# A delta-rule attention and two expert layers in one kernel: key blocks of the first eight items transposed by TensorE instead of by DMA

## The chip, the cores and the metric

One core of one Trainium2 chip runs the whole program. The metric is the device time of one execution in microseconds (us); lower is better. The kernel runs five engines side by side: TensorE (PE in the rows), VectorE (DVE), ScalarE (ACT), GpSimd (POOL), and SyncE (SP), which here only issues DMAs.

## The reference, cut to what matters

```python
def _attn_ref(q, k, v, beta):                # 4 x 8 heads, 768 steps, head size 48
    k_n = k / (norm(k) + 1e-06)
    for t in range(S):
        y[t] = q[t] @ state
        v_old = state applied to k_n[t]
        state = state + beta[t] * outer(k_n[t], v[t] - v_old)

x = y as [3072, 384]
h = x @ w_in;  g = h * clip(h + 3, 0, 6) / 6;  x = g @ w_out      # 384 -> 2048 -> 384
logits = x @ w_gate                          # 8 experts, the best one for each token
out[mask] = gate_w * (relu(x[mask] @ w1[e]) @ w2[e])              # 384 -> 1024 -> 384
```

## The kernel before, in words

The recurrence is computed in chunks of 64 steps. There are 12 chunks (`NS`), and the 32 pairs of batch and head lie in two halves of 16, so there are 24 items (`NI`), item `it` being chunk `it // 2` and half `it % 2`. A half holds eight head numbers `u` of two batches `bb`; `bb` 0 lies on rows 0 to 63 and `bb` 1 on rows 64 to 127. All values go as pairs of a high and a low part (fp16 or fp32r), and each product is made of three matmuls.

For each item, the keys are normalised (`n_stream`, `k_stream`, lines 396 to 435) and written as two 64-column blocks on the diagonal of a tile `Kbd` (128 x 2 x 8 x 128, eight such tiles, `bd_rows` line 373). From `Kbd` come two transposed copies, both by DMA transposes on SP's queue:

- `KTb` (`kt_stream`, line 558), for the products with the queries (`pP`) and with the state (`pR`).
- `KG` (`kg_stream`, line 441), for the product of the keys with themselves. `keysT` (line 437) says where it lies: items 0 and 1 use `KTb`, items 2 and 3 the tiles `QTb`, which no query needs yet, and from item 4 on there is one tile `KG`, so that the transpose of an item waits until the product of the item before has read it.

`g_stream` (line 453) makes the product `pG` of an item with 48 matmuls of 64x64 on two quarters of the array, and ScalarE copies it to `Dt` (four copies) and `MC`. For each group of four items, `t_stream` (line 484) transposes `Dt` on VectorE into `Bt`, scales it, and clears `Xp` in PSUM. `s_stream` (line 501) solves the triangular system of the group on VectorE: 31 steps of two instructions each (`sub`, `Xp`). `z_stream` (line 518) turns the solution into `TT`, and with the products `pZ` into `W2`; `wc_stream` makes `W1`. `chain` (line 677) then carries the state from chunk to chunk (`pR`, `pW`, `pS`), `o_stream` makes the attention output (`pO`), `x_stream` transposes it to `xT`, and `m_stream` (line 877) runs seven of the sixteen slices of the first expert layer on it (`ph`, `py`), while the weights of these slices are converted from 64-bit words by `wi_stream` and `wo_stream` (`nws`; for each piece four operations on VectorE, two on ScalarE and one on GpSimd). The other nine slices, the routing and the second expert layer come after the attention, from about 480 us on (lines 1121 to 1436); the change doesn't touch them.

The order of the work up to there is written out by hand. Each of 31 streams is a generator that yields its instructions in turn; a string `ORDER` (line 959) of 2,998 letters names, letter by letter, the stream whose next entry is emitted, and `drive` (line 926) emits them. A letter stands for one instruction, or for a list of matmuls that belong together. `need` only says which entries must have been emitted earlier; it makes no wait on the chip. Each engine works through its own instructions in this order, and waits where the data need it. `take` hands out one of three PSUM banks. In the string `m` is `g_stream`, `n` is `k_stream`, `c` is `kg_stream`, `d` is `kt_stream`, `l` is `s_stream`, `t` is `m_stream`.

In the trace nearly all of this has the line 36, that of the helper which records each operation, so that the tiles' names tell the instructions apart.

Of the kernel before, what the change touches and what calls it, by code (L numbers as in the profile page):

```python
# [9 lines left out]
FP16 = mybir.dt.float16  # L10
# [61 lines left out]
def kernel(ctx: ExitStack, tc: tile.TileContext, q, k, v, beta, w_in, w_out, w_gate, w1, w2, out):  # L72
# [50 lines left out]
    idq = const.tile([128, 32], FP32, name="idq")  # L123
    onef = const.tile([128, 128], FP32, name="onef")
# [85 lines left out]
    with ExitStack() as ax:  # L210
# [46 lines left out]
        NKG = 1  # L257
        NTT = 1
# [21 lines left out]
        def zero_stream(eng):  # L280
# [7 lines left out]
            yield from need(("K", 3))  # L288
# [99 lines left out]
        def kl_stream():  # L388
            for s in range(NS):
                yield "next"  # L390
                if s > 1:
                    yield from need(("K", 3), ("kn", 2 * s - 4), ("kn", 2 * s - 3))
                ks[s] = yield from load_step(k, s, "kr", 2)
                done.add(("kl", s))
# [42 lines left out]
        def keysT(it):  # L437

            return KTb[it] if it < 2 else QTb[it - 2] if it < 4 else KG[it % NKG]

        def kg_stream():

            for it in range(2, NI):
                yield "next"
                yield from need(("KB", it))
                if it >= NKG + 4:
                    yield from need(("G", it - NKG))
                kb, ktb = Kbd[it % NRK], keysT(it)
                kb.read(it), ktb.write(it)
                yield transposed(ktb, kb)  # L450
                done.add(("K", it))

        def g_stream():

            for it in range(NI):
                g, j = divmod(it, 4)
                yield "next"
                yield from need(("K", it) if it > 1 else ("KT", it))
# [5 lines left out]
                kg = keysT(it)  # L464
                kt = kg.t
                kg.read(it)
                if it >= NMG:
                    yield from need(("Z", it - NMG))
                p = yield from take("pG", kt)
                p_ = p.rearrange("p (u t) -> p u t", t=64)  # L470
                yield [o for u in range(H) for o in halves(lambda r: (p_[r, u], [kt[r, x, u, r] for x in range(2)], [kt[r, x, u, r] for x in range(2)]), True, True)]
                kg.read(it)
# [100 lines left out]
        def ql_stream():  # L573
            for n in range(NS // 2):
                yield "next"
                yield from need(("qf", n - 1) if n else ("K", 3))
# [349 lines left out]
        def drive(streams):  # L926
# [33 lines left out]
            "jjaaaajkjkkkpbrbbbbbbkpbbrqqsrpobsrbrbrbqsbsbqsqrjsqbqqqqnsqrqsosposqr1n1n0nr0onsnosrrnnrsnqrsnnqqso",  # L960
            "osrnqnssnqnsqpdssnrrmssmsnrmsqqnnrdrncmskqmmmmmmjorsqmmsmmrscjqmmkmmskksaomkrmmmrmskmsmmkmksksmassbs",
            "rsrhbrhhbrabarblrbllqrlsbbrlqbspsssrlbbqqlbsbbblb6nnslqlsrsllrlrnnnnllllslnlslsllqslerclnnsmrlsnsnlr",
            "nnsnesrlemllarksllellelllelallslslrbelslbcnnlmmbrlslrmsmlqlaamllresmelrsmlbsmllqlbrebbrlnmlllnllmnlb",
            "crblmisknbrimrmbsmkbbk7fsmmiesibrmemmsqfiscfmq2sbsibimfimsridimmiis3m7i322mhr331h1hf1f1eels20s10qfe1",
            "llsfr031lsl100l60qflf0enr1li2eqninsn10idqelseleliii2in0l1i1ls0i2l41li30l1l40lfe3sngfngql5efgl005l3f1",
            "gs2sc1ls0gnfl1egaa0dl0e1tltnt0s8tnn8lsltl01m0lltetmmpt1lsct0ltntmnmtnmtelpttbttt0sltl1smltl14mfnltlb",
            "ld7s1mtlllc104ltttbtmtlttqtstmqttt1l0ttll1ttmltsm1nntltentststtllmlltt0llqlfaa0nltl0ntfllmbmfqtmmttl",
            "ttqtli10bqtitecstfqtgmg5tpt5tbgmbqmgmitgpqbgtqbmmb7qib2b222bietbmq3biib6tetiq3mt0t0tmt0ttmftt3th02ti",
            "0hqqi0ehttqetttftidl0qt2f3iql0qlqtlllltlin1n1tfeqlnntttttt1tll0elnnll2i4etlelet1l01td1l3tttitl98t24i",
            "1iq31t1tel10nnct3ttntttt0ifllif0i0tfm1ltmt3mnftmn1laa8liilttttimt0tltqd0m0ttlttgmfl0tg1e0gteclfel500",  # L970
            "llq5l1l0efggmltfqg1ltmntdtt1tlpnllltlq08t80lmtnptt4tnllnt4lt1lttltltltttmm1t07tqtqaall1tl0tbl1llltct",
            "0tt1tntl1tll1qlbenttltetttt1nmblntitbiftbtttttmf1ti9mm60ebctqmmmmbtttqt1qq2tttq31bmf2t1t2bttg5itbtgi",
            "ebqq3q52gigg3igtitq030itbmbptbbitmb0imit0mt0i0qp71mnet211eqqt0e0n2qfmteeeenetmt440tt1hh1tef0hd9tqtnt",
            "tqt81fntn08ttqflq0llllfeqllqllltid1tfl21tlqlii0tlt1tit3tt0tltnt1tflttttct2i0300tlit1li3t0ett0tnt1lfi",
            "fllitt0mlillft0tm3lt1qltfl0ntttmnltttldmmtltt1glql5gm5gttgllq4aenablg0fg1tlln0lll1nftm8ttl1tttntltnd",
            "4ttc7tltt11lllmtm1mlmtm0tn1tetlleppblmatlllllcttnttltlt1ltl0qlbttmtt8tlftqtn0ttn1ttlftlqtnitqtft1ttm",
            "t0tttatibqbfqmtmiqbtqbq8ctmmmt1tt1bbttttimiq21t3qitbt69g57igib3i2532egbegitbttgi2qg1pq3emimbi1bmm0b1",
            "e1n0t10mpmtm3t10h02tttheft101hftf1tqqtl3ifllel0tt0telltql0tln4dd10el8qt4eqliqnn2nttte2le1qltfqfel0tt",
            "icltnf1if20l1l0tltitln3tint10ltqtf0l8t0dqntlnfl0llettltttt10mtt0nml0limltmtlmttqitltt0ttn0lll3ttmilt",
            "inetctnttttnnt8llmltllqlttglql5mg5glltt0m9mm10g1l1ttgfmlg1tm1ttllt1t1plplml4qtnlllqttnnttctfn4ltllld",  # L980
# [486 lines left out]
```

## Time and profile before

| | us |
|---|---|
| median of 3 runs | 992.2 |
| lowest, highest run | 988.83, 997.2 |
| the profiled execution, its own time | 993.86 |
| its span in the trace | 992.1 |
| busy: PE, DVE, ACT, POOL | 884.6, 594.8, 568.6, 430.7 |
| PE busy in 0 to 105 us, 105 to 390, 390 to 992 | 34.63, 262.69, 587.27 |
| DVE busy in the same stretches | 94.64, 252.70, 247.47 |

Times in the rows are microseconds from the start of the span unless marked ns. A row of the timeline gives the start, the time to the end of the last of its instructions, the engine, what is written from what, and in brackets how long the engine had sat idle and who released it. `xN` is a count. Rows of matmuls that run one behind the other are merged, so that 48 of them in 1.49 us follow each other every 31 ns, though each one alone is longer. PEclk is the clock granted to TensorE as a share of the full one.

### The profile page before, as it was taken

Reading aid. Unit: us, or ns where it says so; the run is one execution under the profiler, and the core shown is the slowest. Engines: PE = TensorE matmul, PEld = TensorE weight load, DVE = VectorE, ACT = ScalarE, POOL = GpSimd, SP = SyncE. Lnnn points to the kernel's source line nnn. Section 1 sums busy time; section 2 is a strip of 40 time slices with the busy share of each in tenths; the row PEclk is TensorE's granted clock in tenths of the full one; section 3 lists DMA queues with packets and bytes.
Section 4 is the critical chain, followed back from the end, with each engine's and each line's share of the span. In section 5 each row is a group of like instructions: output and inputs, shape, how many; then the busy total and the mean of one; then the engine's idle time right before and its main releaser. Section 6 shows DMA issues by size and latency. Waiting matters only on the chain.

```text
span 992.1 us, 27636 instructions
## 1 busy us (share of the span) xinstructions
PE 884.6 (89%) x11454; PEld 817.0 (82%) x11454; DVE 594.8 (60%) x1612; ACT 568.6 (57%) x1195; POOL 430.7 (43%) x445
## 2 busy tenths in 40 slices
PE   1423898999999999999999999999999999999997
PEld 1323897888888988999778899899899999999996
DVE  7999998988989898564575545554543221222221
ACT  4648888888798877666557333333324452455521
POOL 5354465544646434334343104303105935755751
PEclk9999799999999999999989999999999999999999
DMA  8998888899988875574465323422117634534500
GB/s 144 183 156 162 136 143 146 167 151 181 155 147 175 161 149 150 135 221 157 127 194 180 125 64 100 147 78 98 65 50 269 217 101 147 153 121 131 175 21 21
DMA packets 255080, 138.89 MB, mean 140 GB/s; under 512 B 199587, under 2 KB 239845, under 8 KB 254944
## 3 DMA queue, kind: packets, MB, share of 16 engines
q1 hardware_dynamic: 247120, 118.82, 53.0%
q0 software_dynamic: 7280, 17.41, 5.3%
q8 instruction: 91, 1.49, 0.6%
q10 hardware_dynamic: 544, 0.80, 0.2%
q14 instruction: 45, 0.37, 0.1%
HBM read 71.56 MB, written 35.50 MB: 108 GB/s over the span
## 4 chain that ended last, share of the span: by engine, by line
PE 64%; DVE 18%; issue 6%; ACT 6%; POOL 3%; DMA 1%; SPq 1%; POOLq 0%; ACTq 0%; DVEq 0%
PE ph L1296 11%; PE ph L1087 9%; PE ph L36 7%; PE py L36 6%; PE py L1312 4%; PE py L1311 4%; PE py L1310 4%; PE pz L1075 3%; PE pz L1077 3%; PE pz L1076 3%; PE pO L36 3%; DVE Xp L36 2%; DVE sub L36 2%; PE pW L36 2%; DVE nws L36 1%
## 5 line engine op out<-in xcount | busy, mean ns | idle before, releaser
L1091 DVE SCALAR_TENSOR_TENSOR hL<-ph,hH 128x384 fp32r<-128x384 f32 (+6 forms) x64 | 36.1, 564 | 163.5 <-ACT hH L1090 163.5
L36 POOL TENSOR_TENSOR gL<-t,gH 128x256 fp32r<-128x256 f32 x84 | 64.9, 772 | 129.7 <-ACT gH L36 117.4
L1090 ACT ACTIVATE hH<-ph 128x384 fp32r<-128x384 f32 (+6 forms) x64 | 31.7, 495 | 105.2 <-PE ph L1087 105.2
L36 PE MATMUL ph<-xTH,wiH 128*128 128x256 f32 x252 | 76.9, 305 | 14.4 <-DVE t L36 13.7
L1299 ACT ACTIVATE t<-ph,half 128x512 f32<-128x512 f32 x54 | 37.2, 689 | 78.0 <-PE ph L1296 77.8
L1256 POOL DMA_INDIRECT slots<-row,di x24 | 23.9, 997 | 125.1 <-DVE di L1248 119.6
L1300 DVE SCALAR_TENSOR_TENSOR t<-t,ph 128x512 f32<-128x512 f32 x54 | 37.1, 687 | 66.7 <-ACT t L1299 66.4
L1075 PE MATMUL pz<-a2H,hH 128*128 128x384 f32 (+1 forms) x216 | 73.2, 339 | 0.4 <-ACT hH L1090 0.4
L1076 PE MATMUL pz<-a2L,hH 128*128 128x384 f32 (+1 forms) x216 | 72.4, 335 | 0.0
L1077 PE MATMUL pz<-a2H,hL 128*128 128x384 f32 (+1 forms) x216 | 72.4, 335 | 0.0
L1108 POOL DMA_INDIRECT out_dram<-yo,rw x29 | 28.0, 966 | 100.6 <-ACT yo L1107 96.4
L36 PE MATMUL ph<-xTL,wiH 128*128 128x256 f32 x252 | 70.6, 280 | 0.0
L36 PE MATMUL ph<-xTH,wiL 128*128 128x256 f32 x252 | 70.6, 280 | 0.0
L36 PEld LDWEIGHTS ph<-xTH,wiH 128*128 128x128 f32 x252 | 47.5, 189 | 24.4 <-DVE t L36 24.1
L1304 DVE TENSOR_TENSOR gL<-t,gH 128x512 fp32r<-128x512 f32 x54 | 46.6, 863 | 32.7 <-ACT gH L1303 32.5
L36 DVE TENSOR_TENSOR Xp<-Xp,sub 128x31 f32<-128x31 f32 (+15 forms) x186 | 63.7, 342 | 2.4
L36 PE MATMUL py<-woH,gH 128*128 128x392 f32 x168 | 63.5, 378 | 1.1 <-ACT gH L36 1.1
L36 DVE TENSOR_TENSOR sub<-Bt,Xp 128x31 f32<-128x31 f32 (+15 forms) x186 | 61.7, 332 | 2.8 <-POOL Bt L36 0.5
L148 POOL TENSOR_TENSOR a2L<-r,a2H 128x384 fp32r<-128x384 f32 x64 | 62.5, 1007 | 0.0
L148 POOL TENSOR_TENSOR a1L<-r,a1H 128x512 fp32r<-128x512 f32 x48 | 60.4, 1300 | 0.1
L36 PE MATMUL py<-woH,gL 128*128 128x392 f32 x168 | 58.2, 346 | 0.5 <-POOL gL L36 0.5
L1087 PE MATMUL ph<-yTL,a1H 128*128 128x384 f32 (+5 forms) x168 | 58.3, 347 | 0.0
(321 smaller groups left out, 3122.4 us busy)
## 6 DMA issues: line engine op xcount, KB each, us to landing
r<-in_moe_w_dram SPq DMA_DIRECT2D x32, 768.0 KB, 4.5
slots<-zrow SPq DMA_DIRECT2D x8, 784.0 KB, 6.4
stage<-in_moe_w_in_dram SPq DMA_DIRECT2D x16, 384.0 KB, 3.9
stage<-in_moe_w_out_dram SPq DMA_DIRECT2D x16, 384.0 KB, 3.4
row<-ypart SPq DMA_DIRECT2D x6, 784.0 KB, 4.3
ysave<-row SPq DMA_DIRECT2D x6, 784.0 KB, 3.6
rw<-slots SPq DMA_DIRECT2D x24, 196.0 KB, 3.1
kr<-in_k_dram SPq DMA_DIRECT2D x24, 192.0 KB, 4.2
```

Of the source, the lines that this page charges most:

```text
L36: return self.fn(*self.a, **self.k)
L148: in_order(pool.tensor_tensor(dst[1], src_ap, dst[0].bitcast(FP32), ALU.subtract))
L1075: pe.matmul(o, hh[:, ts_], a2[0][:, fp], start=fp == 0, stop=False)
L1076: pe.matmul(o, hh[:, ts_], a2[1][:, fp], start=False, stop=False)
L1077: pe.matmul(o, hl[:, ts_], a2[0][:, fp], start=False, stop=fp == KF2 - 1)
L1087: pe.matmul(ph, a1[a][:, c, fs], xt[x][:, c, 0:n], start=k == 0, stop=k == 3 * KD - 1)
L1296: pe.matmul(ph, wi(a, f)[:, c], xt[x][:, c], start=n == 0, stop=n == 3 * KD - 1)
L1299: act.activation(t_, ph, ACTF.Relu, bias=half, scale=1.0 / 6.0)
L1304: dve.tensor_tensor(gL, t_, gH.bitcast(FP32), ALU.subtract)
L1310: pe.matmul(o, gh[:, ts_], wo(0, fp), start=fp == 0, stop=False)
L1311: pe.matmul(o, gh[:, ts_], wo(1, fp), start=False, stop=False)
L1312: pe.matmul(o, gl[:, ts_], wo(0, fp), start=False, stop=fp == NF2 - 1)
```

## The change

Items 0 to 7 no longer get a DMA-transposed copy for `pG`. Instead, `pt_keys` transposes the 32 blocks of 64x64 of an item's `Kbd` on TensorE (fp16, against a 64x64 identity `id16` that ScalarE copies out of `ident` at the start) into one PSUM bank, and ScalarE copies them with one instruction (128 x 1024, fp16) into one half of `KG`. The halves alternate, so that item `it` waits for the product of item `it - 2`. `kg_stream` begins with item 8 and always uses the whole of `KG`. Six DMA transposes go; the 24 into `KTb` and those of items 8 to 23 stay. Where the transposed keys of item 3 had to be emitted before further loads and clears, its `Kbd` has to be now, and the first transposes of the queries need no longer follow the products of items 2 and 3. The list `ORDER` is another one: 3,008 letters, with 16 more of `m` and 6 fewer of `c`, and the other letters in other places.

```diff
+    id16 = const.tile([128, 64], FP16, name="id16")
+    for hb in range(2):
+        r = slice(64 * hb, 64 * hb + 64)
+        act.activation(id16[r], ident[r, r], ACTF.Copy)
...
         NKG = 1
+        NPT = 8
...
-            yield from need(("K", 3))
+            yield from need(("KB", 3))
...
-        def keysT(it):
-
-            return KTb[it] if it < 2 else QTb[it - 2] if it < 4 else KG[it % NKG]
-
         def kg_stream():
 
-            for it in range(2, NI):
+            for it in range(NPT, NI):
                 yield "next"
                 yield from need(("KB", it))
-                if it >= NKG + 4:
-                    yield from need(("G", it - NKG))
-                kb, ktb = Kbd[it % NRK], keysT(it)
+                yield from need(("G", it - 1), *([("G", it - 2)] if it == NPT else []))
+                kb, ktb = Kbd[it % NRK], KG[0]
                 kb.read(it), ktb.write(it)
                 yield transposed(ktb, kb)
                 done.add(("K", it))
 
+        def pt_keys(it):
+
+            kb = Kbd[it % NRK]
+            kb.read(it)
+            kc = KG[0].t[:, it % 2].rearrange("p u c -> p (u c)").rearrange("p (x u c) -> p x u c", x=2, c=64)
+            p = yield from take("pT", kb.t)
+            p_ = p.bitcast(FP16).rearrange("p (x u c) -> p x u c", x=2, c=64)
+            ops = []
+            for u in range(H):
+                for x in range(2):
+                    for bb in range(2):
+                        r = slice(64 * bb, 64 * bb + 64)
+                        ops.append(PE.transpose(p_[r, x, u], kb.t[r, x, u, r], id16[r]))
+            yield ops
+            if it > 1:
+                yield from need(("G", it - 2))
+            yield ACT.activation(kc, p_, ACTF.Copy)
+            give(p)
+            return kc
+
         def g_stream():
...
-                yield from need(("K", it) if it > 1 else ("KT", it))
+                yield from need(("K", it) if it >= NPT else ("KB", it))
...
-                kg = keysT(it)
-                kt = kg.t
-                kg.read(it)
+                if it < NPT:
+                    kc = yield from pt_keys(it)
+                    key = lambda r, u: [kc[r, x, u] for x in range(2)]
+                else:
+                    kc = KG[0].t
+                    KG[0].read(it)
+                    key = lambda r, u: [kc[r, x, u, r] for x in range(2)]
...
-                    yield from need(("O", 4 * n - 2 + bp), ("Q", 4 * n - 2 + bp)) if n else need(("G", 2 + bp))
+                    yield from need(("O", 4 * n - 2 + bp), ("Q", 4 * n - 2 + bp)) if n else need()
...
         ORDER = [
-            "jjaaaajkjkkkpbrbbbbbbkpbbrqqsrpobsrbrbrbqsbsbqsqrjsqbqqqqnsqrqsosposqr1n1n0nr0onsnosrrnnrsnqrsnnqqso",
-            "osrnqnssnqnsqpdssnrrmssmsnrmsqqnnrdrncmskqmmmmmmjorsqmmsmmrscjqmmkmmskksaomkrmmmrmskmsmmkmksksmassbs",
...
+            "jjjkarrabjjjkkkbbaaspppbbbbbskbqsrbsrbrqbrsbqbsssqbqrobnsqqqqqssopqnnqrrqon0nrrnq1mr0snmnnsqsos1msnn",
+            "msnrmmsnsmsmnmnrnmmssosmsnsronqommmnmmkdrmmnmoaaprrbmmjrsrrrksmmmkkmkspskkkkaabrsrmbmmksksrbbsobmrqm",
...
```

## Rows read from the trace of the kernel before

**Rows 1.** The page: busy time of each engine

```profile
PE 884.6 (89%) x11454; PEld 817.0 (82%) x11454; DVE 594.8 (60%) x1612; ACT 568.6 (57%) x1195; POOL 430.7 (43%) x445
```

**Rows 2.** Windows: stretch, time, then busy of PE, PEld, DVE, ACT, POOL; PEclk

```profile
0.00:105.00 105.00, 34.63 (x721) 30.86 (x722) 94.64 (x258) 66.16 (x146) 50.06 (x54) 1.00 0.90 160
105.00:390.00 285.00, 262.69 (x6284) 244.24 (x6281) 252.70 (x778) 239.83 (x519) 143.50 (x142) 0.97 0.86 158
390.00:992.00 602.00, 587.27 (x4458) 541.86 (x4456) 247.47 (x579) 262.60 (x532) 237.19 (x250) 0.99 0.41 128
...
45.00:100.00 55.00, 17.50 (x383) 15.81 (x382) 53.50 (x150) 35.79 (x77) 24.94 (x25) 1.00 0.89 158
...
75.00:100.00 25.00, 10.29 (x268) 9.36 (x269) 24.26 (x66) 20.73 (x43) 11.36 (x9) 1.00 0.87 162
```

**Rows 3.** Waits of PE, 0 to 100 us: us in total, times, longest

```profile
PE pG L36 <- DMA KG<-Kbd: 9.4, 2, 7.7
...
PE pG L36 <- DMA QTb<-Kbd: 3.9, 1, 3.9
```

**Rows 4.** Waits of DVE, 0 to 45 us

```profile
DVE Kbd L36 <- ACT Kbd L36: 1.3, 1, 1.3
...
DVE nws L36 <- ACT nws L36: 0.9, 2, 0.7
...
DVE uL L36 <- ACT uH L36: 0.4, 1, 0.4
```

**Rows 5.** Waits of DVE, 45 to 100 us (the whole answer)

```profile
DVE W L36 <- ACT W L36: 0.2, 1, 0.2
```

**Rows 6.** The chain that ended last, 49 to 66 us: start, us, what

```profile
57.40 4.92 DMA KG<-Kbd
```

**Rows 7.** Timeline, the first group's keys up to its solve

```profile
6.39 0.52 ACT L36 ACTIVATE vsq<-kr 128x384 f32<-128x384 f32 x1 [4.08 <-DMA kr<-in_k_dram]
...
17.35 0.87 PE L36 MATMUL pwt<-ident,nws 128*128 128x128 f32 x3 [2.41 <-DVE eiv L36]
...
21.81 0.56 DVE L36 TENSOR_TENSOR Kbd<-kn,Kbd 64x384 f16<-64x384 f32 x1
...
40.48 1.49 PE L36 MATMUL pG<-QTb 64*64 64x64 f16 x48 [3.88 <-DMA QTb<-Kbd]
...
42.01 1.54 ACT L36 ACTIVATE Dt<-pG 32x256 f32<-32x256 f32 x4 [1.73 <-PE pG L36]
...
44.90 1.23 DVE L36 STREAM_TRANSPOSE Bt<-Dt 128x1024 f32<-128x1024 f32 x1
...
46.18 1.01 ACT L36 ACTIVATE Xp<-onef 128x1024 f32<-128x1024 f32 x1
```

**Rows 8.** Timeline, 84 to 130 us: a copy, a collision, a product

```profile
84.19 1.25 DVE L36 STREAM_TRANSPOSE Bt<-Xp 128x1024 f32<-128x1024 f32 x1
...
85.47 1.95 ACT L36 ACTIVATE TT<-Bt 128x1024 f16<-128x1024 f32 x1 [0.30 <-DVE Bt L36]
...
87.56 2.73 POOL L36 TENSOR_TENSOR TT<-Bt,TT 128x1024 f16<-128x1024 f32 x1 [2.43 <-ACT TT L36]
...
87.68 2.65 DVE L36 TENSOR_SCALAR s<-s 128x32 f32<-128x32 f32 x1
...
124.17 0.95 PE L36 MATMUL pG<-KG 64*64 64x64 f16 x48
```

**Rows 9.** Tiles KG and s: min/median/max ns of one, first and last start

```profile
L36 PE MATMUL pG<-KG x960: 186/193/260, 62.4 to 344.0; 64*64 64x64 f16 x192
L36 SPq DMA_TRANSPOSE KG<-Kbd x20: 1795/2886/4812, 57.4 to 336.3; - x20
...
L36 DVE TENSOR_SCALAR s<-s x18: 159/180/2647, 12.4 to 290.7; 128x32 f32<-128x32 f32 x18
```

**Rows 10.** Waits of ACT, 45 to 100 us

```profile
ACT nws L36 <- DMA stage<-in_moe_w_in_dram: 1.2, 1, 1.2
```

More of the change, by code (lines that the diff above doesn't have):

```diff
@@ L391, in kl_stream @@
                 if s > 1:
-                    yield from need(("K", 3), ("kn", 2 * s - 4), ("kn", 2 * s - 3))
+                    yield from need(("KB", 3), ("kn", 2 * s - 4), ("kn", 2 * s - 3))
                 ks[s] = yield from load_step(k, s, "kr", 2)
@@ L463, in g_stream @@
                     Dts[g] = Dt
-                kg = keysT(it)
-                kt = kg.t
-                kg.read(it)
+                if it < NPT:
[5 more added lines that the diff above has]
+                    key = lambda r, u: [kc[r, x, u, r] for x in range(2)]
                 if it >= NMG:
                     yield from need(("Z", it - NMG))
-                p = yield from take("pG", kt)
+                p = yield from take("pG", kc)
                 p_ = p.rearrange("p (u t) -> p u t", t=64)
-                yield [o for u in range(H) for o in halves(lambda r: (p_[r, u], [kt[r, x, u, r] for x in range(2)], [kt[r, x, u, r] for x in range(2)]), True, True)]
-                kg.read(it)
+                yield [o for u in range(H) for o in halves(lambda r: (p_[r, u], key(r, u), key(r, u)), True, True)]
                 done.add(("G", it))
@@ L575, in ql_stream @@
                 yield "next"
-                yield from need(("qf", n - 1) if n else ("K", 3))
+                yield from need(("qf", n - 1) if n else ("KB", 3))
                 qrs[n] = tmp([128, B, H, D], FP32, "qr")
@@ L965 @@
[L965 to L979, printed above, removed]
@@ new lines @@
+            "3s0fgalfattlslstil0el21tmn0dsi0ltl1tmnlil0ltstttml10mmtmcf01pttlfntt0t0pl11ttlmlbelntl1l1llsndnets0m",
+            "mqnnlttlmt1tl1t4qclltt41tne7blllltmltla1lnsmalqlmtttstntttmsltmn0slmtml0t1bmtl1ttqtttlesm0tlbl8l1lql",
+            "qltl0itfetttm0cbtmiqtt10btfbtf8sittgb5tmt5qbgqqgmgq2b2qbi22ggib3bibmmmitb3ibt0m0t0mtqt3nthtit7ftif03",
+            "tth60ttptph2ife0eieteiel1t0t0tnlltlnt1el0qltl1tll08ld412elqnttq1l4t9tnnltf1ttt2ltteqleelq0l0tc1fl0nt",
+            "nfetiltttedalifl1l0t1lttt1tlntilnftltlitmtmct8tmtimlmmf2tlqlmlia0q303tideten0lttitt1tt1f0ilq01fitttt",
@@ new lines @@
+            "0gg3lmg0tt51nlnq0lllqm3nlmqmllmlpp1tm5gtmqllg1gbl1t4fn4tlltt1cbnqltt1ttflt0bttl1llmt1qltmtm7tnla0ean",
+            "llt1lltttttmll8tltltttlmtttfn0ti1tfbdtettt8nt1tti0btmqtqtitbtfttmtbtceq1i0bt33t1i3it2qi6bqitttttt12m",
+            "qtmbm0mm9mtbbttq1qmgb5gqgbt5tigq223bb0ntgqthqip70fhgtitittt0ti0eeei010thi0tllnl0lli0tllnptt2t20l11li",
+            "nttetndtqtttttf4fillftlle0qtftt1t801cdttt3l10n421qtlle01lnfqtntalql2n3m01mfl0tmmnate1tltft0llttqt10m",
+            "cl3tqfnt0etle1ql0lmb1ttqltmtttlte0ql3nt0lmmmnllmqmtln19tt8tdmitimpnptltieqttnlqtgbtig5tlt5ilglgglg8a",
@@ L990 @@
+            "tittft8ttttti1tt3tt8ttttgg32i55ig2i1ittgte1tegg1t8010tdt2ttt1t0t7tttt1fii01t1tfttittttfttt30tfi9t31t",
+            "ttiditttettttttttt1uuu43tfu1ttut0ut100uf2tttut4u8utttttfuut83tttttu0tfggu55gttg1t0gug01utttt1ttuttuf",
+            "0tuutttttutuuut1ft90tttttuttutt10ttuttuutftt11tuttfttett14tutttt8tt8t41uttttut8tt1tutttutttug5g5tggg",
+            "ttttguuttt8uututtuttttutuuuttuutuutttttutttttutttuttuuttutttutttuttttttutttuttt9ttt88tuttututtutttuu",
+            "tutttut9",
         ]
```

27 lines of the change are left out of this document (14 added, 13 removed).

## The prediction, made before the changed kernel ran

> **What bounds the kernel now.** I read the page first, then the windows, then the waits of two engines, then the timeline of the first 45 us, and the chain last. The page shows TensorE busy for 89% of the span and VectorE for 60% [rows 1], which reads as if TensorE were the bound throughout. The windows show that it isn't: in the first 105 us TensorE works 34.63 us and VectorE 94.64; from 105 to 390 all three big engines are at 84 to 92% (PE 262.69, DVE 252.70, ACT 239.83 of 285), and from 390 on TensorE fills 587.27 of 602 [rows 2]. So the end is set by when TensorE is brought into full work, and by the stalls between 105 and 390; and when it is brought in is set by VectorE.
>
> The waits that the change takes away are TensorE's. Up to 100 us it waited 9.4 + 3.9 = 13.3 us for transposed keys before `pG` [rows 3]. A reader who stops here would book 13.3 us. But TensorE has 70 us of idle time there anyhow. VectorE waited for no such DMA: between 45 and 100 us the whole list of its waits is 0.2 us [rows 5], and it was busy 53.50 of 55 us [rows 2]. The chain does pass through one of these transposes for 4.92 us [rows 6]; yet VectorE had work during all of that time, so taking the transpose out of the chain leaves another chain of nearly the same length, made of VectorE's own instructions. That is why I don't read the gain from the chain.
>
> **The change part by part.** The sum goes against the profiled execution, 993.86 us, which is 1.66 above the median of 992.2.
>
> *The wait for transposed keys in the first group.* Item 3's product started at 40.48 us after 3.88 us of waiting for its DMA [rows 7]. ScalarE's last copies of it ended at 43.55, and VectorE's transpose of `Dt` started at 44.90, because VectorE was working on other entries up to then. In the new list I count VectorE's entries ahead of the landmarks (each letter is one entry, and the order of a stream's own entries is in the code). Ahead of the transpose of `Dt` stand 92 entries before and 96 after. The first entry of the solve is number 100 in both lists; the transpose of the solved `Xp`, which is at 84.19 us [rows 8], is number 208 in both; the transpose of the second group's `Dt` is number 241 in both. So nothing of VectorE's work moves out of the way, and only its waits can go. Before 45 us it waited 1.3 + 0.9 + 0.4 = 2.6 us for ScalarE's parts of the keys, weights and values [rows 4]; its other waits there are for the first load of the keys, which stays. Ends: 0 and -2.6. I take -2.0, as with the products done earlier ScalarE's copies of the first group are spread out and the list was made with that in hand. From 45 to 100 us there is 0.2 us to win; I take 0.
>
> *The transposes added on TensorE.* 8 items of 32 blocks of 64x64. The nearest row is `pG`, also 64x64 fp16 on the same two quarters: 48 in 1.49 us at 40.48 us, 31 ns apart, and 48 in 0.95 us at 124.17 us, 20 ns apart [rows 7, 8]. 32 of them take 0.63 to 1.0 us an item, 5 to 8 us in all. The far end is the transpose of the weights, 3 of 128x128 fp32 in 0.87 us, 0.29 us each [rows 7], which makes 9.3 us an item and 74 us in all. I take 1.0 us an item, since size, type and quarters are those of `pG`. In the new list item 7's transposes stand before VectorE's entry number 217, so before about 88 us, and all of them are in the 70 idle us: cost 0. Without that cover they would cost 8 us.
>
> A single `pG` matmul is listed with 186 to 260 ns [rows 9] though one starts every 31 ns [rows 7]: length and spacing are different things here. [...] No row of the kernel before shows an fp16 transpose.
>
> *The copies added on ScalarE.* 8 copies of 128x1024. The nearest row is the clearing of `Xp`, the same size, 1.01 us [rows 7]; the far end is `TT`, the same size from fp32 with reordered reads, 1.95 us [rows 8]. The new copy reads and writes in order, so I take 1.0: 8 us in all. Up to 105 us ScalarE works 66.16 us [rows 2], so 39 are free. Between 75 and 100, however, it is at 20.73 of 25 [rows 2], and two copies (items 6 and 7) fall there or just before; queued behind a copy that waits for its transposes are ScalarE's halves of `Kbd`, `W` and `Qs`, for which VectorE and GpSimd wait. Ends: 0 and the full 2 x 1.0 = 2.0. I take +0.5. The two copies that make `id16` stand where ScalarE sits idle for 4.08 us until the first keys land [rows 7]: 0.
>
> *The DMA transposes removed.* Six, at a median of 2.886 us each on SP's queue [rows 9], so 17 us of that queue. Behind them are the loads of k, v, q and weight stages. Whoever uses these hardly waits: ScalarE 1.2 us at most between 45 and 100 [rows 10], VectorE nothing [rows 5]. Ends 0 and -1.2; I take 0, as VectorE is the one that matters.
>
> *The edits of `need`, the halves of `KG`, the bank for `pT`.* `need` makes no wait on the chip. The queries' first transposes, now free of items 2 and 3, are issued long after these anyway. A third user of the three PSUM banks holds one for about 2 us an item, in a stretch in which TensorE is idle two thirds of the time. Ends -0.5 and +1; I take 0.
>
> *The rest of the list.* From the second group on nothing but the order changes. Entry numbers of VectorE at the transposes of the solved `Xp`, groups 1 to 5: 375, 541, 713, 880, 1031 before and 375, 537, 711, 881, 1030 after. The first attention output comes after 270 instead of 285 entries and the first `ph` after 296 instead of 310, 14 entries earlier; at 94.64 us for 258 instructions [rows 2], 0.37 us each, that is 5 us. But the second chunk's first `ph` comes after 406 instead of 402, so that this lead is given back within one chunk. I take 0, with -5 as the end. A part that no count shows is collisions: VectorE's `s` took 2.65 us at 87.68 us where its median is 0.18, and it ended when GpSimd's 2.73 us on `TT` ended [rows 8, 9]. Another order draws these anew; two such events either way, 5 us, stay in the range.
>
> Sum: -2.0 + 0.5 + 0 = -1.5 against the profile, so 992.4 there and 990.7 at the median. I say 990.5.
>
> **The rivals.**
>
> *Faster: TensorE comes into work earlier and keeps the lead.* The whole 2.6 us of waits goes, the 5 us of the first `ph` stay, and the collisions fall out well (-5): 992.2 - 12.6 = 980. For it: from 105 us on TensorE is the fullest engine, and has 22.3 us of idle time between 105 and 390 that could go [rows 2]. Against it: the landmarks of the later groups hardly move.
>
> *Slower: the transposes don't overlap.* If each takes the 0.29 us of the weights' transposes, an item needs 9.3 us of transposes, 1.0 of copy and 1.5 of product, 11.8 in all. The first item's `Kbd` ends at 22.4 us [rows 7]; four items later it is 69.6, plus 1.5 for the copies to `Dt` 71.1, where VectorE's transpose of `Dt` started at 44.90. The solve and all behind it come 26 us later: 992.2 + 26 = 1018. It decides from the point where an item's transposes exceed (44.9 - 22.4 - 1.5) / 4 - 2.5 = 2.7 us, 85 ns each. Against it stands the spacing of `pG`.
>
> *Slower: the new list stalls more.* Half as much idle time of TensorE again between 105 and 390, +11: 1003. Nothing in the counts speaks for it, except that ScalarE has 8 us more to do beside a full VectorE.
>
> *The wait only changes its name.* `pG` is issued earlier, but its readers on ScalarE and VectorE take it up where they did before, and even the 2.6 us stay: 992 to 993. The equal entry numbers speak for it.
>
> **How the numbers follow.** My forecast has 0.52, the changed name 0.16, the faster rival 0.22, the transposes that don't overlap 0.04, the stalling list 0.06. A difference of less than about 1%, 10 us, can't be told from no change here. The first two are within it: same 0.68; faster 0.22; slower 0.10. The range reaches down to the faster rival, 979 (980 less 1 for its rounding), and up to 992.2 + 2.0 for the copies + 5 for collisions + 1 for the banks = 1000, to which I add 1 towards the stalling list: 1001. Out of it are the transposes that don't overlap and most of the stalling list, and the outer part of the faster rival.
>
> **What would show it right or wrong.** Right: no `pG` waits for a DMA before 100 us, and TensorE waits for VectorE or ScalarE instead; VectorE is still busy 53 of 55 us between 45 and 100; the transpose of the first solved `Xp` starts between 81 and 85 us (84.19 before); 32 transposes span 0.6 to 1.0 us, a copy takes 1.0; the last of the six such transposes of `Xp` starts within 4 us of its old place near 390. Wrong: the first solve starts more than 4 us earlier or later than before; the transposes span more than 2.7 us an item; or TensorE's idle time between 105 and 390 differs from 22.3 us by more than 5.

## The result: 1.2% faster, and the profile after

The changed kernel took 979.27 us (median of 4 runs, 978.67 to 981.2); the kernel before, run beside it, 990.8 (4 runs, 988.83 to 997.2). The ratio is 0.9876 [0.9827, 0.9925]: faster by 0.75 to 1.7%, at the lower end of the range, and not the "same" that was forecast. The profiled execution took 979.62 us with a span of 977.8, 14.3 us shorter than the one before.

The page's busy times, to be read against [rows 1]:

```profile
PE 886.0 (91%) x11710; PEld 819.7 (84%) x11710; DVE 583.5 (60%) x1612; ACT 574.1 (59%) x1205; POOL 431.8 (44%) x445
```

TensorE has its 256 transposes more, ScalarE ten instructions more. The row to stop at is VectorE's: the same 1612 instructions, 11.3 us less busy time. GpSimd did the same 445.

The windows after, with the columns of [rows 2]; the last runs to the start of the second solved `Xp`:

```profile
0.00:105.00 105.00, 49.05 (x1149) 43.72 (x1151) 93.31 (x282) 78.42 (x167) 53.10 (x56) 1.00 0.72 134
105.00:390.00 285.00, 262.73 (x6384) 245.54 (x6377) 248.89 (x762) 242.29 (x525) 145.44 (x143) 0.99 0.85 160
...
45.00:100.00 55.00, 27.95 (x667) 25.52 (x667) 51.66 (x165) 43.10 (x87) 30.18 (x28) 1.00 0.57 110
0.00:136.90 136.90, 77.93 (x1832) 70.62 (x1833) 124.53 (x377) 108.08 (x233) 72.68 (x77) 0.99 0.77 139
```

The same window of the kernel before:

```profile
0.00:146.70 146.70, 72.52 (x1588) 66.47 (x1589) 134.93 (x378) 101.56 (x223) 71.68 (x78) 0.95 0.88 154
```

Up to 105 us VectorE was through 282 instructions instead of 258 in about the same busy time. Call X1 the start of VectorE's transpose of the second group's solved `Xp`, entry 375 of VectorE in both lists. It came at 136.93 us instead of 146.7. VectorE's busy time up to there fell by 134.93 - 124.53 = 10.4 us; its idle time stayed, 11.8 before and 12.4 after; GpSimd's busy time stayed too, 71.68 and 72.68. The last `pO` of the attention ended at 459.61 instead of 470.7. So of 14.3 us of span, 9.8 are gained up to X1, 1.3 between X1 and the last `pO`, and 3.2 behind it. There the change touches nothing, but TensorE was busy for 509.21 us before and for 506.24 after on the same work; the granted clock of the whole profile is 0.983 before and 0.993 after. These 3.2 us are not put down to the change; the other 11.1 are near the 11.5 between the medians.

Where the 10.4 us lie is seen when VectorE's groups up to X1 are set side by side, shapes kept apart (count, busy us, mean ns of one, idle before). The kernel before:

```profile
L36 DVE TENSOR_SCALAR s<-s 128x32 f32<-128x32 f32 x9 | 4.8, 539 | 0.1
L36 DVE COPY W<-TT 32x512 f16<-32x512 f16 x8 | 3.7, 466 | 0.0
...
L36 DVE SCALAR_TENSOR_TENSOR uL<-vr,sgv,uH 128x384 f16<-128x384 f32 x4 | 3.4, 859 | 0.4 <-ACT uH L36 0.4
L36 DVE TENSOR_TENSOR kn<-kr,rn 128x384 f32<-128x384 f32 x4 | 3.0, 752 | 0.1
L36 DVE TENSOR_SCALAR bY<-bX 128x192 f32<-128x192 f32 x1 | 1.4, 1448 | 0.0
L36 DVE TENSOR_SCALAR bX<-bX 128x192 f32<-128x192 f32 x1 | 1.1, 1053 | 0.0
```

The changed kernel:

```profile
L36 DVE SCALAR_TENSOR_TENSOR uL<-vr,sgv,uH 128x384 f16<-128x384 f32 x4 | 2.4, 602 | 0.0
L36 DVE COPY W<-TT 32x512 f16<-32x512 f16 x8 | 2.2, 278 | 0.1
L36 DVE TENSOR_TENSOR kn<-kr,rn 128x384 f32<-128x384 f32 x4 | 2.2, 555 | 0.1
L36 DVE TENSOR_SCALAR s<-s 128x32 f32<-128x32 f32 x9 | 1.5, 168 | 0.0
...
L36 DVE TENSOR_SCALAR bY<-bX 128x192 f32<-128x192 f32 x1 | 0.3, 263 | 0.0
L36 DVE TENSOR_SCALAR bX<-bX 128x192 f32<-128x192 f32 x1 | 0.2, 250 | 0.0
```

Same forms, same counts, shorter: 17.4 us against 8.8 in these six groups, 8.6 of the 10.4. VectorE did not do less; the same instructions took less. That they were held by GpSimd's, that is, ended only with the GpSimd instruction beside them, is seen one by one in the two traces. Up to X1, 17 VectorE instructions of the kernel before took over 0.3 us more than the shortest of their form in either trace, 15.2 us more in all; in the changed kernel 8 did, 5.6 us in all. Every one of the 25 overlaps a GpSimd instruction, and 22 start inside one and end with it or within 0.5 us behind it. The difference, 9.6 us, is nearly all of the 10.4. The prediction had seen one such hold, `s` in 2.65 us beside GpSimd's 2.73 us on `TT` [rows 8]. In the changed kernel the same two instructions don't meet. Its timeline there:

```profile
81.78 0.55 DVE L36 TENSOR_REDUCE ss<-ksq 128x8 f32<-128x384 f32 x1
82.25 0.55 DVE L36 SCALAR_TENSOR_TENSOR nws<-stage,nws 128x384 int32<-128x384 int32 x1
84.02 0.55 DVE L36 TENSOR_REDUCE ss<-ksq 128x8 f32<-128x384 f32 x1 [1.23 <-ACT ksq L36]
...
82.81 2.73 POOL L36 TENSOR_TENSOR TT<-Bt,TT 128x1024 f16<-128x1024 f32 x1 [2.12 <-DVE nws L36]
```

While GpSimd works from 82.81 to 85.54, VectorE waits for ScalarE and reduces, and the reduction at 84.02 takes its usual 0.55 us. The Trainium skill, "SBUF — State Buffer", section "Who interferes with whom", states that VectorE and GpSimd share one pair of ports, that whichever instruction starts first has it to its end while the other is blocked, that VectorE's copies, casts and `tensor_scalar` can be so blocked, and that on trn2 its `tensor_reduce` never is. The two timelines agree: 2.65 us against 0.18 for the one kind, 0.55 as always for the other.

Of the waits, TensorE's between 0 and 100 us (us in total, times, longest), against [rows 3]:

```profile
PE pG L36 <- ACT KG L36: 9.3, 4, 5.7
PE pT L36 <- ACT Kbd L36: 7.1, 3, 5.0
PE pG L36 <- DVE nws L36: 5.0, 1, 5.0
```

No `pG` waits for a DMA any more; the first two rows, 16.4 us of waits for ScalarE, stand where 13.3 us of waits for DMAs stood (14.6 with 1.3 for the DMAs into `KTb`). VectorE's up to 45 us, against [rows 4]:

```profile
DVE ss L36 <- ACT vsq L36: 5.0, 2, 3.4
...
DVE Kbd L36 <- ACT Kbd L36: 0.4, 1, 0.4
DVE nws L36 <- ACT nws L36: 0.2, 1, 0.2
```

And between 45 and 100 us, against [rows 5]:

```profile
DVE ss L36 <- ACT ksq L36: 1.8, 2, 1.2
DVE uL L36 <- ACT uH L36: 0.2, 1, 0.2
```

The added work itself, from the tile `KG` (min, median, max ns of one) and from the timeline:

```profile
L36 ACT ACTIVATE KG<-pT x8: 1000/1012/1023, 22.4 to 82.6; 128x1024 f16<-128x1024 f16 x8
```

```profile
23.47 1.49 PE L36 MATMUL pG<-KG 64*64 64x64 f16 x48 [1.31 <-ACT KG L36]
24.77 1.04 PE L36 MATMUL pT<-id,Kbd 64*64 64x64 f16 x32
```

### The profile page after: what moved, and what is told of

The parts are those of the page before. It is cut to its first block, busy times and chain, and to the rows that moved or that the text cites. A ratio compares the mean times of both kernels' runs of the same rounds, so it can differ in the third digit from the quotient of the medians.

```text
span 977.8 us, 28163 instructions
## 1 busy us (share of the span) xinstructions
PE 886.0 (91%) x11710; PEld 819.7 (84%) x11710; DVE 583.5 (60%) x1612; ACT 574.1 (59%) x1205; POOL 431.8 (44%) x445
## 5 line engine op out<-in xcount | busy, mean ns | idle before, releaser
L36 PE MATMUL ph<-xTH,wiH 128*128 128x256 f32 x252 | 76.1, 302 | 14.6 <-DVE t L36 14.5
L36 PEld LDWEIGHTS ph<-xTH,wiH 128*128 128x128 f32 x252 | 47.6, 189 | 22.9 <-DVE t L36 22.7
L36 PE MATMUL py<-woL,gH 128*128 128x392 f32 x168 | 57.4, 342 | 1.0 <-issue 1.0
```

The lines of the kernel that those rows point to most:

```text
L36: return self.fn(*self.a, **self.k)
```

## The experiments

Two factors were changed at once, the transposes and the list, so these were first taken apart. Then two questions: does VectorE's time up to X1 set the end, and is it GpSimd that lengthens VectorE's instructions? In each, X1 and VectorE's busy time up to it are read from the windows and the timeline. Compare with 146.7 and 134.93 for before, 136.9 and 124.5 for after. Traces are of one execution each; times are medians.

### The transposes without the list

`e1_old_list_pe`: the change with the letters in the old order.

```diff
         ORDER = [
-            "jjjkarrabjjjkkkbbaaspppbbbbbskbqsrbsrbrqbrsbqbsssqbqrobnsqqqqqssopqnnqrrqon0nrrnq1mr0snmnnsqsos1msnn",
+            "jjaaaajkjkkkpbrbbbbbbkpbbrqqsrpobsrbrbrbqsbsbqsqrjsqbqqqqnsqrqsosposqr1n1n0nr0onsnosrrnnrsnqrsnnqqso",
...
```

> The code of the changed kernel with the list of the kernel before: where the list had a DMA transpose of items 2 to 7, the transposes on TensorE and the copy stand instead (for items 0 and 1 where their transposes into KTb stand), no earlier than behind the last entry of the item before; everything else is in the old order. Theory A (the gain is the new order, by which VectorE runs into GpSimd's instructions less often; the transposes themselves save only waits of an idle TensorE): 986 to 996 us, VectorE busy near 595 us, the second transpose of Xp near 146 us. Theory B (the gain is the DMA transposes taken away): 978 to 983 us, the second transpose of Xp near 137 us.

Measured: 1003.21 us, ratio 1.0115 [1.0077, 1.0154]; X1 154.7, VectorE busy 131.8, idle 22.9. Neither theory's numbers hold. VectorE's and TensorE's waits up to 100 us:

```profile
DVE MC L36 <- ACT MC L36: 6.6, 4, 2.6
DVE nws L36 <- ACT nws L36: 3.5, 2, 2.8
```

```profile
PE pG L36 <- ACT KG L36: 27.4, 7, 12.7
```

In the old list each product stands a DMA's length behind its keys. Transposes, copy, product and the copies of the product now follow each other through TensorE's and ScalarE's queues there, and VectorE meets `MC` before ScalarE has made it.

`e11_old_list_pe_own`: the same, but the transposes are a stream of their own, begun where the old list began the DMA, the copy three entries later.

```diff
+        def pt_stream():
+            for it in range(NPT):
+                yield "next"
+                yield from need(("KB", it))
+                KCs[it] = yield from pt_keys(it)
+                done.add(("K", it))
...
-                    kc = yield from pt_keys(it)
+                    kc = KCs[it]
```

> The old list with TensorE's transposes as a stream of their own, put where the old list starts the DMA transposes, and the copies from PSUM three entries later, so that they don't stand behind the item before's copy of MC in ScalarE's queue as in the first of these runs (1003.2). If that run lost its time by the serial chain of transposes, copy, product and copies: VectorE's idle time up to X1 back to 12 to 16 us, X1 142 to 148, kernel 982 to 993. Rival (the eight added copies on ScalarE stand in front of what VectorE waits for wherever they are put under this list): idle time 18 to 24 us, X1 150 to 155, kernel 996 to 1004.

Measured: 1000.26 us, 1.0077 [1.0045, 1.0108]; X1 152.9, busy 128.8, idle 24.1 (just outside the rival's 18 to 24). The rival's times hold: under the old list the time is lost in both places tried for the transposes. That the added copies cause it wherever they are put is not shown by two places. Its windows show where the time goes, VectorE having worked 22.89 us of 25 to 50 us before, and 23.73 after:

```profile
25.00:50.00 25.00, 12.03 (x331) 10.94 (x331) 14.57 (x44) 17.05 (x38) 6.71 (x6) 0.94 0.63 122
```

### The list without the transposes

`e2_new_list_dma` (DMA transposes as early as the new list lets them be) and `e3_new_list_dma_later` (at the places where the change has its transposes on TensorE): the new order, `kg_stream` as it was, and the same relief in `need`.

```diff
-            yield from need(("K", 3))
+            yield from need(("KB", 3))
...
-                yield from need(("qf", n - 1) if n else ("K", 3))
+                yield from need(("qf", n - 1) if n else ("KB", 3))
```

> The code of the kernel before, with its DMA transposes, in the order of the new list: each DMA transpose stands as early as its data allow (behind the item's Kbd, from item 5 on also behind the product of the item before), the transposes of items 0 and 1 into KTb are pulled ahead to there, and the transposes on TensorE and their copies are left out. Theory A (order): 978 to 985 us, the second transpose of Xp at 137 to 141 us, VectorE busy near 584 us. Theory B (transposes): 986 to 996 us, the second transpose of Xp near 146 us. In between, if the products stand so close behind Kbd in the new list that a DMA of some 5 us no longer fits: TensorE and ScalarE wait for KG, 984 to 988.

> As e2_new_list_dma, but each DMA transpose stands where the new list has the item's transposes on TensorE, so later in SP's queue, behind the loads of weights that it held up there. In e2 and in three other kernels the time from the first ph to the last attention output pO was 348 to 350 us, so theory C says that the time of the first ph sets the end. Theory C here: whatever the first ph does, the last pO comes 347 to 351 us behind it. For the transposes: if e2 lost its time to loads behind the transposes in SP's queue, the first ph comes at 112 to 122 us and the kernel takes 981 to 992 us; if it lost it because the new order leaves no room for a DMA between Kbd and product, the first ph stays behind 126 us and the kernel takes 993 us or more.

Measured: the first 998.06 us, 1.0054 [1.0036, 1.0073], X1 159.5, busy 127.2, idle 32.3, slower than each of the three ranges named for it; the second 988.99 us, 0.9966 [0.9948, 0.9985], X1 150.5, busy 128.1, idle 22.4. The second's time lies in the range named for loads held up in SP's queue, and its first `ph`, at 122.56 us, just behind it; the range for a lack of room lies farther off. In the second, VectorE's and ScalarE's waits up to 100 us:

```profile
DVE nws L36 <- ACT nws L36: 9.2, 4, 5.3
```

```profile
ACT nws L36 <- DMA stage<-in_moe_w_in_dram: 10.9, 3, 6.1
```

The new list wants its weights early, and their loads stand behind the DMA transposes in SP's queue; ScalarE waits for the loads, VectorE for ScalarE. In the first, whose transposes stand earlier in that queue, the same wait of ScalarE is 19.8 us; in the changed kernel it is 4.8. So the four corners, as X1 = busy + idle of VectorE: before 134.9 + 11.8; transposes alone 131.8 + 22.9; list alone 128.1 + 22.4; both 124.5 + 12.4. The busy time falls in each of the other corners. Only the two together get it without ten more microseconds of waits.

### Does the time up to X1 set the end?

An alternative was that the first `ph`, where TensorE comes into full work, sets it. `e6_old_ph_earlier` moves 22 entries of the old list, 12 of them VectorE's, behind the first `ph`.

```diff
-            "llsfr031lsl100l60qflf0enr1li2eqninsn10idqelseleliii2in0l1i1ls0i2l41li30l1l40lfe3sngfngql5efgl005l3f1",
-            "gs2sc1ls0gnfl1egaa0dl0e1tltnt0s8tnn8lsltl01m0lltetmmpt1lsct0ltntmnmtnmtelpttbttt0sltl1smltl14mfnltlb",
+            "llsfr031lsl100l60qflf0enr1li2eqninsn10idqelselelii2n0l11ls02l4l30ll40lfe3sngfngq5efg53fgs2scsgnfegaa",
+            "detltntiiii1i1ll00l11l0l10l010s8tnn8lsltl01m0lltetmmpt1lsct0ltntmnmtnmtelpttbttt0sltl1smltl14mfnltlb",
```

> The kernel before, DMA transposes and all, with 22 entries of its list, 12 of them VectorE's, moved from in front of the first ph to right behind its matmuls: the last W2 of the first group, parts of the second chunk's chain, and six steps of the second solve. The first ph needs none of them. Theory C (what stands ahead of the first ph on VectorE sets the end): the first ph at 116 to 119 us instead of 122.3, the last pO 347 to 351 us behind it, the kernel 985 to 990 us against 992. Rival D (the prediction's: such a lead is given back within a chunk): the first ph earlier, the last pO within 1.5 us of 470.7, the kernel 991 to 994 us.

Measured: 997.29 us, 1.0057 [1.0029, 1.0085]. Neither theory's range holds. The first `ph` came 4.0 us earlier (118.26 for 122.31), X1 4.7 later (151.4), the last `pO` 5.2 later (475.94). VectorE's work up to X1 was the same (134.3 us), its waits 5.3 us longer. The end followed X1, not the first `ph`.

`e7_new_before_ph` and `e8_new_after_ph` add 14 VectorE instructions on zeros to the changed kernel, ahead of the first `ph` or behind it, both ahead of X1.

```diff
+        def extra_stream():
+            for _ in range(14):
+                yield "next"
+                yield DVE.tensor_scalar(zrow[:, 0:384], zrow[:, 0:384], 1.0, None, ALU.mult)
```

> The changed kernel with 14 more instructions on VectorE, zeros times one on 128x384 (some 0.36 us each), spread between the transpose of the first solved Xp and the first ph: as many as the new list has fewer there. Theory C: the first ph 4 to 7 us later than 109.2, the last pO 347 to 351 us behind it, the kernel 983 to 987 us. Rival D: the first ph later, but the last pO within 1.5 us of 459.6, the kernel 978 to 981 us.

> The changed kernel with the same 14 instructions on VectorE spread behind the first ph, up to the transpose of the second solved Xp. Theory C in its strict form: first ph at 109 us and last pO within 1.5 us of 459.6, the kernel 978 to 981 us, since behind the first ph VectorE's load is no longer what counts. Rival E (VectorE sets the pace up to 140 us and beyond): the last pO 3 to 6 us later, 982 to 986 us.

Measured: 983.86 us (0.9891 [0.9852, 0.9929]) and 984.6 (0.9902 [0.9866, 0.9938]), against 979.27 and 0.9876 without them: by the medians 4.6 and 5.3 us more, by the ratios 1.5 and 2.6 (0.0015 and 0.0026 of 991), with intervals that overlap. The times alone would not settle it; the traces do. The first `ph` came at 115.5 in the one and at 109.04 in the other (109.24 without), X1 at 143.1 and 143.7, the last `pO` at 466.57 and 464.6, so 7.0 and 5.0 us later than without. Where X1 is alike the end is alike, to within 2 us; the first `ph` lies 6.5 us apart in the two, and the end doesn't follow it.

X1 is not the whole of it. From X1 to the end of the last `pO` it is 323.2 to 325.0 us in the kernels with the old list (329.3 in `e11_old_list_pe_own`), but 317.7 to 323.5 in those with the new one. `e3_new_list_dma_later` has its X1 3.8 us later than the kernel before and is still the faster by 0.3%, with its last `pO` at 469.2. So X1 tells the end to within some 6 us, with the old list more closely; what makes the rest, behind X1, isn't shown.

### Is it GpSimd?

`e4_new_pool_more` adds 12 GpSimd instructions on zeros to the changed kernel between 48 and 137 us.

```diff
+        def extra_stream():
+            for _ in range(12):
+                yield "next"
+                yield POOL.tensor_tensor(zrow[:, 0:384], zrow[:, 0:384], zrow[:, 0:384], ALU.add)
```

> The changed kernel with 12 more instructions on GpSimd, zeros added to zeros on 128x384, spread over the list between the first solve's start and the end of the second (some 48 to 137 us). GpSimd is busy little more than half of that stretch, and nothing waits for their result. Theory A (VectorE's instructions are held while GpSimd's run): VectorE's busy time up to 390 us grows by 3 to 8 us though it has the same instructions, and the second transpose of Xp moves from 136.9 to 140 to 146 us; the kernel takes 982 to 988 us. Rival (GpSimd's time is free as long as it has idle time): within 1.5 us of the changed kernel in all three.

Measured: VectorE's busy time up to X1 128.05, 3.5 more on the same 377 instructions, and X1 139.6, 2.7 later. One group of it:

```profile
L36 DVE TENSOR_SCALAR s<-s 128x32 f32<-128x32 f32 x9 | 3.6, 397 | 0.0
```

So GpSimd's work lengthens VectorE's, 168 ns to 397 here. The busy time up to 390 us grew by 3.2, within theory A's range; X1 fell just short of it. The kernel took 980.18 us (0.9879 [0.9841, 0.9916]), 0.9 more, which can't be told from nothing and is what the rival had; the last `pO` came 0.4 later, so what was lost was made up behind X1.

The other way round, `e5_old_pool_less` and `e9_old_pool_less2` take 21 GpSimd subtractions out of the kernel before, so that the low parts of these weights are left out of the result. The one clears the low parts with GpSimd at the start, the other with ScalarE.

```diff
-                yield from split_ops([x[:, :, f * 128:(f + 1) * 128] for x in wi], t_.rearrange("p (c f) -> p c f", c=KD))
+                yield ACT.activation(wi[0][:, :, f * 128:(f + 1) * 128], t_.rearrange("p (c f) -> p c f", c=KD), ACTF.Copy)
...
-                yield from split_ops([x[:, 0:DM] for x in do], t_)
+                yield ACT.activation(do[0][:, 0:DM], t_, ACTF.Copy)
...
-                yield from split_ops([x[:, DM:YW] for x in do], wc)
+                yield ACT.activation(do[0][:, DM:YW], wc, ACTF.Copy)
```

> The kernel before without GpSimd's subtractions that make the low parts of the first seven slices' weights (21 instructions, left out of the list; these low parts stay zero from two clears on GpSimd at the start, so that the products with them add nothing but are still made). Theory A: in the trace before, VectorE's longest instructions up to 70 us ended with these, so VectorE's busy time up to 147 us falls by 3 to 6 us and the second transpose of Xp comes at 140 to 144 us instead of 146.7; the kernel takes 985 to 988 us. Rival (GpSimd is off the path): the second transpose of Xp within 1.5 us of 146.7.

> The kernel before without GpSimd's 21 subtractions that make the low parts of the first seven slices of the MLP weights; those low parts are left at zero by four copies with scale 0.0 on ScalarE at the very start, so the first seven slices are multiplied in their high parts alone. Theory (the end is set by when VectorE gets through its entries up to the second solve, and GpSimd's instructions beside it hold VectorE's): VectorE's busy time up to the start of the second solve's X falls by 3 to 5 us on the same instructions, with no later start this time; X1 142 to 144, last pO 324 to 325 us behind it, kernel 986 to 989. Rival (GpSimd's load beside VectorE doesn't set the pace; the changed kernel's gain is of its order alone): X1 within 1.5 us of 146.7, kernel 990 to 993.

Measured: the first 991.21 us, 0.9993 [0.9968, 1.0018]; busy 131.5 (-3.4), but the clears delayed the first group (its `Dt` was transposed at 47.23 us, before at 44.90), and X1 is 146.1. Inconclusive for the kernel's time. The second 988.72 us, 0.9966 [0.9944, 0.9988]; X1 144.0, and its window:

```profile
0.00:144.00 144.00, 71.86 (x1588) 65.89 (x1588) 129.47 (x377) 106.89 (x227) 55.70 (x58) 0.96 0.89 156
```

16.0 us less of GpSimd give VectorE 5.5 us back, of which 2.7 reach X1; the other 2.8 became waits (idle 14.5 instead of 11.8). The busy time fell by more than the theory's 3 to 5, X1 lies at the weak end of its range, and the last `pO` and the kernel's time came as it had them.

`e12_old_tt_quarters` leaves GpSimd its work and only cuts the instruction behind the longest hold.

```diff
-                yield POOL.tensor_tensor(tt[:, :, 1], xt_, tt[:, :, 0], ALU.subtract)
+                yield [POOL.tensor_tensor(tt[:, j, 1], xt_[:, j], tt[:, j, 0], ALU.subtract) for j in range(4)]
```

> The kernel before with one edit: each group's GpSimd subtraction that makes the low part of TT (128x1024, 2.73 us) is made in four quarters (128x256, some 0.7 to 0.8 us each) in the same place of the list. Theory (a VectorE instruction that meets a GpSimd one is held until that one ends, so the longest single hold, s of 128x32 in 2.65 us, is as long as what is left of the subtraction): that s takes 0.4 to 0.9 us, VectorE's busy time up to X1 falls by 1.5 to 2.5 us from 135.0, X1 144.5 to 146, kernel 988 to 991. Rival (the hold is a matter of how much GpSimd has to do there, not of the length of its instruction): the held time only moves to the instructions behind s, VectorE's busy time up to X1 within 1 us of 135.0, X1 within 1 us of 146.7, kernel 990 to 993.

The timeline at that place, to be read against [rows 8]:

```profile
88.04 0.74 DVE L36 TENSOR_SCALAR s<-s 128x32 f32<-128x32 f32 x1
88.70 0.35 DVE L36 TENSOR_SCALAR nws<-nws 128x384 int32<-128x384 int32 x1
90.64 0.42 DVE L36 SCALAR_TENSOR_TENSOR MC<-pG,MC 128x256 f16<-128x256 f32 x1 [1.59 <-ACT MC L36]
...
87.93 3.35 POOL L36 TENSOR_TENSOR TT<-Bt,TT 128x256 f16<-128x256 f32 x4 [2.43 <-ACT TT L36]
```

The mechanism is shown: the hold shrinks from 2.65 to 0.74 us, what is left of a quarter. Its price is not what the theory had. VectorE goes on, and two instructions later waits 1.59 us for ScalarE's `MC`, which the long hold had covered. A part of the hold also moved, as the rival had it: the copy `W` from `TT`, at 91.70 us, took 1.49 us beside GpSimd's `Qs`, where it had taken 0.84. Busy time up to X1 133.5 (-1.4, just short of what was expected), idle 13.7, X1 147.2, 0.5 later than before and within the rival's range; 990.51 us, 0.9987 [0.9965, 1.0008]: no gain. A hold is worth only what it reaches beyond the next wait.

### A version that may beat both

`e10_new_identities_pool` gives twelve small set-up instructions of VectorE to GpSimd; `e13_new_tt_quarters` has the quarters of `TT` besides.

```diff
-                yield DVE.tensor_scalar(idq[32 * x:32 * x + 32], ident[32 * x:32 * x + 32, 32 * x:32 * x + 32], C12, None, ALU.mult)
+                yield POOL.tensor_scalar(idq[32 * x:32 * x + 32], ident[32 * x:32 * x + 32, 32 * x:32 * x + 32], C12, None, ALU.mult)
...
-                        yield DVE.tensor_copy(w_[i].pr[0][r, :, r], idq[r].unsqueeze(1).to_broadcast([32, H, 32]))
+                        yield POOL.tensor_copy(w_[i].pr[0][r, :, r], idq[r].unsqueeze(1).to_broadcast([32, H, 32]))
```

> The changed kernel with twelve small VectorE instructions of the set-up of the solves (four scalings of the identity, eight copies of it into W, some 2.9 us together) given to GpSimd. Theory (VectorE's load up to 140 us sets the end): X1 1.5 to 3 us earlier than the changed kernel's 136.9, kernel 976 to 978.5. Rival (GpSimd's instructions hold VectorE by as much as they take from it): X1 within 1 us of 136.9 or later, kernel 979 to 982.

> The changed kernel with the twelve set-up instructions given to GpSimd (976.8 in an earlier run) and also each group's subtraction for TT in four quarters. Theory: up to X1 no VectorE instruction of the changed list was held by this subtraction (VectorE made reductions and waited for ScalarE beside it), so X1 stays within 1 us of 135.5 and the kernel at 975 to 978. Rival (long GpSimd instructions hold VectorE everywhere): VectorE's busy time up to X1 1.5 us or more lower, kernel below 975.

Measured: 976.75 us (0.9851 [0.982, 0.9881]) with X1 at 135.5, and 976.34 us (0.9844 [0.981, 0.9878]) with X1 at 135.7. X1 is 1.4 us earlier than the changed kernel's, just short of what was expected; the times are as expected. Both are faster than the kernel before by 1.5%. That they beat the changed kernel by 2.5 to 2.9 us isn't shown, since the intervals overlap with its own. The quarters added nothing where nothing was held, as the theory had it.

## Why the prediction was wrong

*VectorE bounds up to 105 us: right*, and beyond it, up to X1 near 140 us: with either list, most edits ahead of X1 moved the end with it (`e4_new_pool_more` is the exception, 2.7 us at X1 and 0.4 at the last `pO`). The waits that the change takes off TensorE were not where the gain lay.

*"Nothing of VectorE's work moves out of the way, and only its waits can go": the step that failed.* Equal entry numbers were taken for equal time. The numbers were right (375 at X1 in both), but the same entries took 10.4 us less, and the waits, which alone were given a gain (-2.0), didn't shrink at all (11.8 us, then 12.4). The three waits named for it did fall by just that, from 2.6 to 0.6 us; but the wait for ScalarE's `vsq`, one of those that were to stay, grew from 2.9 to 5.0. The collisions had a paragraph of their own, and were taken at 0 with 5 us at either end. Measured, VectorE's instructions up to X1 are shorter by 8.6 us in the six groups shown. The term could have been sized before: the mean of each form in the windows up to X1 stood in the trace (`s` 539 ns by a median of 180, `bY` 1448). That sum says how much can be lost to holds, 15.2 us in the 17 longest, and so how lopsided a new draw is: the change and the four other kernels with one of the two edits (the first two pairs of experiments) all lost less (busy time 3.1 to 10.4 us lower), while `e6_old_ph_earlier`, which only moved 22 entries, has 0.7 less.

*The removed DMA transposes, taken at 0 (ends 0 and -1.2): mis-sized.* The price was read under the old list, where between 45 and 100 us ScalarE waited 1.2 us for loads and VectorE not at all. Under the new list they cost 150.5 - 136.9 = 13.6 us at X1, 10.0 of it idle time of VectorE, and 9.7 us by the medians.

*The copies on ScalarE, +0.5 (at most 2.0): right in the pair, not alone.* They take 1.01 us each, as assumed. Under the old list the transposes with these copies cost 8.0 us at X1 (154.7 for 146.7), an end that the sum had excluded by treating the two edits one by one.

*The transposes on TensorE: right.* 32 in 1.04 us, just above the 0.6 to 1.0. Each is listed with 238 ns (median of 256), yet 32 in 1.04 us is one every 33 at most. The Trainium skill, "TensorE: Matmul & The Clock Gate", Part 4: PE-mode transpose, gives about 275 ns for one of 128x128 bf16 inside a kernel; that is near the length here, and far from the spacing. The granted clock was 1.00 up to 105 us, with all 256 transposes in that stretch.

*"The lead of the first `ph` is given back": half right.* It came 13.1 us earlier, not 5, and was not the point: `e6_old_ph_earlier` moved it forward and the end went back, and `e7_new_before_ph` and `e8_new_after_ph` have it 6.5 us apart with medians 0.7 us apart.

*The signs named beforehand* spoke clearly. The first solve's transpose was to start between 81 and 85 us and started at 79.39, 4.8 earlier than before, where over 4 was named as a sign of being wrong; VectorE was to be busy 53 of 55 us and was for 51.66, with 1.8 us of waits for ScalarE's `ksq`; the last `Xp` came at 378.5 instead of near 390. Only TensorE's idle time between 105 and 390 stayed as named, 22.3 us.

*The faster rival* had the right size, 980, of other terms: it gave 2.6 to the waits and 5 to the first `ph`, measured as nothing, and 5 to the collisions, which brought about twice that. That the range, which ends at this rival, holds 979.27 is luck: its lower end was added up from the wrong terms.

What stays open: how much of each single hold reaches the end, and why a change of list draws fewer. Removing one (the quarters) or 21 possible ones (the weights' subtractions) from the old order gave 0 and 2.7 us at X1, as ScalarE's parts weren't ready; the new order's waits are about as long in all as the old one's, but no run put single holds back into it at their old places.

## What to carry to other kernels

Before an order of instructions is called equal because as many stand ahead of a landmark, sum the engine's time there form by form: count times (mean less the shortest usual) is what it loses to its neighbour, and where VectorE is busy for 134.9 of 146.7 us beside a busy GpSimd, that loss is part of the bound. Price two edits that were made for each other as a pair: here each alone was worth between +10.4 and -2.4 us by the medians, both together -11.5. And before a stall or a hold is removed, look at what its engine meets next; the 2.65 us hold hid a wait of 1.59 us, and cutting it won nothing.

## What the runs showed of the hardware

Some VectorE instructions that start inside a GpSimd one are held to the end of it, small ones too: `s`, 128x32, took 2.65 us beside a 2.73 us instruction, 0.74 beside quarters, 0.17 alone. `bX`, `bY`, `kn`, the copies of `W` and `tot`, of 128x1, were held so too. Others run at their usual length. Of the solve's `sub` and `Xp`, which read or write PSUM, 28 in the kernel before and 30 in the changed one started up to X1 inside a GpSimd instruction that had over 0.3 us more to go than they need, and none took more than 0.06 us beyond its shortest; nor were the reductions held, or scalings of one column such as `elv`. The kernel before:

```profile
61.62 0.40 DVE L36 TENSOR_TENSOR sub<-Bt,Xp 128x231 f32<-128x231 f32 x1
101.77 0.15 DVE L36 TENSOR_SCALAR elv<-eiv 128x1 int32<-128x1 int32 x1
...
61.36 0.91 POOL L36 TENSOR_TENSOR Kbd<-kn,Kbd 64x384 f16<-64x384 f32 x1 [1.15 <-ACT Kbd L36]
100.31 2.38 POOL L36 TENSOR_TENSOR Bt<-Bt,bY 128x1024 f32<-128x1024 f32 x1 [6.54 <-DVE nws L36]
```

So an overlap is not always a hold; the form of the instruction matters. GpSimd's clears hold too: `bY` took 1.45 us at 36.55 beside GpSimd's clear of `Qs` (36.08 to 37.88), which only writes, and 0.26 in the changed kernel at 34.18, after that clear had ended. GpSimd paid for the cut itself: four quarters took 3.35 us where the whole took 2.73, and 3.16 in `e13_new_tt_quarters`.

In `e11_old_list_pe_own` the granted clock was 0.50 and 0.57 between 50 and 100 us, with TensorE busy 8.40 and 9.37 of each 25 us, where `e1_old_list_pe` had 1.00. VectorE did as much there in both (24.34 and 21.72 us busy, against 24.38 and 21.29), so its pace shows no loss from TensorE's half clock in that stretch. What the clock cost the kernel isn't shown: the two lists differ, and this profiled execution, 1004.68 us, is the slowest of the five.
